# Half rows of a projection weight on 128 partitions, one output DMA, three idle products

## The chip, the cores and the metric

The kernel runs on one core of one Trainium2 chip. Its five engines are TensorE (PE), VectorE (DVE), ScalarE (ACT), GpSimd (POOL) and SyncE (SP); 16 DMA engines move data between HBM and the on-chip memory SBUF. The metric is the device time of one execution in microseconds (us), as the median of several runs.

## The reference

Two independent problems, A and B, are computed, and their outputs are laid side by side. Each is one decode step of attention over the last 4,096 positions of a cache, with a projection before and one behind it. All inputs are bf16.

```python
B, Sq, D = 2, 1, 576
Hq, Hkv, Sk, Dh = 32, 16, 16384, 128
W = 4096
q = (x @ wq).reshape(B, Sq, Hq, Dh).transpose(0, 2, 1, 3)      # wq: 576 x 4096
k = repeat(k_cache[:, :, Sk - W:, :], 2, axis=1)               # 16 heads, each used by two of q
v = repeat(v_cache[:, :, Sk - W:, :], 2, axis=1)
p = softmax(einsum("bhqd,bhkd->bhqk", q, k) * Dh ** -0.5)
o = einsum("bhqk,bhkd->bhqd", p, v)
out = o.transpose(0, 2, 1, 3).reshape(B, Sq, Hq * Dh) @ wo     # wo: 4096 x 576
return concatenate([out_A, out_B], axis=-1)
```

For one query position a head, nearly all bytes are those of K and V: 16 slabs of K and 16 of V, 4 MB each. With wq and wo of both problems the kernel reads 153 MB.

## The kernel before, in words

**Slabs and the ring.** `stream` is the order in which big loads are issued: wq of A and of B, then K and V slabs by turns. A slab is 128 partitions of 32 KB, and `ring` has 4 slots. `issue_slab` puts one slab on SyncE's DMA queue; from the fifth on, SyncE first waits until the last reader of the slot is done (`reader`). The loads of wo (`issue_wo`) go between them on the same queue; the last V slab is cut in two (`PIECES`), and the last rows of wo go out in three DMAs (`issue_last`, semaphores `wl_sem`) behind it. The outputs follow last.

**The order of work.** The Python code adds operations to one list for each engine (`S.add(engine, function, dependencies, tag)`). Each engine runs its list in order. Dependencies become semaphore waits in front of an operation, and those that an earlier wait already covers are dropped. Nothing is reordered, so the order of the calls in the code is the order on the engine.

**The q phase.** wq has 576 rows. Of these, 512 are loaded as a slab in which partition p holds rows 4p to 4p+3 (four chunks), and the last 64 (`DREM`) go into `wqr`. Before the change, row r of problem P lies in partition 2r+P, 8 KB each (L248), so that both problems together fill 128 partitions; `x_dup` holds each of x's last 64 values twice, with zeros (by `maskP`) where the partition belongs to the other problem (L361). `f_xT` (L355) transposes x, chunk by chunk, on PE into a bank of PSUM, and `f_xev` (L369) spreads it into `xT` on ACT. `do_qpair` (L421, with repeated weights L170) then runs the products of q for two groups of heads at a time: 5 chunks by 4 banks, four times. `do_qrow` evicts them on ACT (L435, L440), DVE and ACT rearrange them, and GpSimd builds `zq`, the weights of the score products.

**Steady state.** For each K slab DVE transposes it in four parts (L485), PE makes scores (L510), maxima and exponentials follow on DVE, PE and ACT, and PE multiplies the V slab of an earlier step (L601).

**The tail.** The last V slab comes in two pieces. Between and behind its products PE runs idle products into a bank that is no longer read (`idle_out`): two behind `redist` by `do_redist(D_ // 2, 2)`, and two by `keep_on(2)`, the first of them L729, the others L170. Then come the combination of the accumulator (L648), a normalisation on DVE (L683), the last products with wo (L760; `fin_ops` is a DVE copy, L783, that they wait for), and two copies to `out_sb` (`do_E`: ACT L792 for the lower half of the columns, DVE L793 for the upper). `do_out` (L801) issues the output: A's rows from SyncE long before, B's lower half from ACT and its upper half from SyncE. SyncE then waits until all outputs have landed (L955).

Of the kernel before, what the change touches and what calls it, by code (L numbers as in the profile page):

```python
# [6 lines left out]
BF16 = mybir.dt.bfloat16  # L7
ACTF = mybir.ActivationFunctionType
ALU = mybir.AluOpType
AX = mybir.AxisListType  # L10
# [49 lines left out]
def build_kernel(nc, probs, out, cfg=None):  # L60
    cfg = dict(cfg or {})
    NR = cfg.get("NR", 4)
# [26 lines left out]
    HH = HD // 2  # L89
    NXC = NFC + 1  # L90
    NOUT = wo0.shape[1]
# [15 lines left out]
    with es:  # L107
        sb = lambda name, shape, dt: es.enter_context(nc.sbuf_tensor(name, shape, dt))
        ring = sb("ring", [128, NR, SLABW], BF16)
        xt = sb("xt", [128, NKT, 2048], FP32)  # L110
        wqr = sb("wqr", [128, HD], BF16)
        wob = sb("wob", [128, 2, 8, NOUT], BF16)
        xT = sb("xT", [128, NXC, NPROB, 128], BF16)
        x_dup = sb("x_dup", [NPROB * Bb, DREM, NPROB], BF16)
        maskP = sb("maskP", [NPROB * Bb, NPROB], BF16)
        x_sb = sb("x_sb", [NPROB * Bb, D], BF16)
# [45 lines left out]
        wo_sem = [sem("wo%d" % r) for r in range(2)]  # L162
        x_sem = [sem("xload%d" % P) for P in range(NPROB)]
        wl_sem = [sem("wl%d" % n_) for n_ in range(len(HEADS))]
# [19 lines left out]
        def load_x(P, eng):  # L184
            return dma_op(eng, x_sem[P], 1, lambda e: e.dma_start(
                x_sb[P * Bb:(P + 1) * Bb, :], probs[P][0][:, 0, :]).then_inc(x_sem[P], 16), [], "xload%d" % P)
        x_dma = {0: load_x(0, "act")}
# [56 lines left out]
        def issue_wq(n, P):  # L244
            wqP = probs[P][3]
            r = n % NR
            deps = [reader[n - NR]] if n >= NR else []
            wq_dma[P] = dma_op("sp", wq_sem, 1, lambda e: e.dma_start(  # L248
                wqr[P::NPROB, :], wqP[NFC * 128:D, :]).then_inc(wq_sem, 16), [], "wqr%d" % P)
            slab_dma[n] = dma_op("sp", ring_sem[r], 1, lambda e: e.dma_start(  # L250
                ring[:, r, :], wqP[0:NFC * 128, :].rearrange("(p s) n -> p (s n)", s=NFC)).then_inc(ring_sem[r], 16), deps, "wq%d" % P)

            if P == 0:
                for P_ in range(1, NPROB):
                    x_dma[P_] = load_x(P_, "sp")
# [90 lines left out]
        def f_xT(e, bank):  # L346
            last = None
            bb = bank[:].bitcast(BF16)
            NB = NPROB * Bb
            for ch in range(NXC):  # L350
                if ch < NFC:
                    src = x_sb[0:NB, 0:NFC * 128].rearrange("b (p s) -> b s p", s=NFC)[:, ch, :]
                else:
                    src = x_dup[0:NB, :, :].rearrange("b r t -> b (r t)")
                last = e.transpose(bb[:, ch * NB:(ch + 1) * NB], src, ident_b[0:NB, 0:NB])  # L355
            return last
        issue_until(0)
        init_small()
        init["maskP"] = S.add("dve", lambda e: e.tensor_reduce(
            maskP[:], ident_b[0:NPROB * Bb, 0:NPROB * Bb].rearrange("d (p b) -> d p b", b=Bb), AX.X, ALU.max), [p_ident_b], "maskP")  # L360
        x_cd = S.add("dve", lambda e: e.tensor_tensor(  # L361
            x_dup[:], x_sb[:, NFC * 128:D].unsqueeze(2).broadcast_to([NPROB * Bb, DREM, NPROB]),
            maskP[:].unsqueeze(1).broadcast_to([NPROB * Bb, DREM, NPROB]), ALU.mult), [init["maskP"]] + list(x_dma.values()), "xdup")

        n_x, bank_x, op_xT = tb_job(f_xT, "xT", list(x_dma.values()) + [x_cd, p_ident_b])

        def f_xev(e):
            NB = NPROB * NXC
            return e.activation(  # L369
                xT[:].rearrange("c h p (a w) -> c (h p) a w", a=4)[:, :, :, 0:Bb],  # L370
                bank_x[:].bitcast(BF16)[:, 0:NB * Bb].rearrange("c (p b) -> c p b", b=Bb).unsqueeze(2).broadcast_to([128, NB, 4, Bb]),
                ACTF.Copy)
        op_xev = S.add("act", f_xev, [op_xT, p_zxT], "xev")
        tb_consumer[n_x] = op_xev

# [20 lines left out]
        def do_qpair(i):  # L396
# [4 lines left out]
            banks = q_banks(i)  # L401
            order = [NFC] + list(range(NFC))
            if Gs[0] % GPP:
                order = order[::-1]
            todo_ = [(ch, b) for ch in order for b in range(4)]
            seen = {b: 0 for b in range(4)}
# [3 lines left out]
            for g in range(2):  # L410
                def fn(e, part=todo_[(0, ends[0])[g]:ends[g]]):
                    last = None
                    for ch, b in part:
                        c0 = (b % 2) * HH + 512 * (Gs[b // 2] % GPP)
                        w_ = ring[:, nq % NR, ch * HD + c0:ch * HD + c0 + 512] if ch < NFC else wqr[:, c0:c0 + 512]
                        start, stop = seen[b] == 0, seen[b] == NFC
                        seen[b] += 1
                        if q_first[0] == (P, ch):
                            last = matmul_again(e, q_first[1], banks[b], w_, start, stop, False)
                        else:  # L420
                            last = q_first[1] = e.matmul(banks[b], xT[:, ch, P, :], w_, start=start, stop=stop)  # L421
                            q_first[0] = (P, ch)
                    return last
                op = S.add("pe", fn, [slab_dma[nq], op_xev] + list(wq_dma.values()) + prev, "q%d" % Gs[g])
                reader[nq] = op
                q_done[Gs[g]] = op
# [268 lines left out]
        def do_redist(G, idle=0):  # L695
# [14 lines left out]
            if idle:  # L710
                def f_idle(e):
                    r = None
                    for _ in range(idle):
                        r = matmul_again(e, last[0], idle_out, maskB[:, :], True, True)
                    return r
                S.add("pe", f_idle, [chain[(ND - 1, "exp")], init["maskB"]], "idle%d" % G)
            redist[G] = op
# [7 lines left out]
        fin_ops = []  # L725

        def keep_on(n):
            def f(e):
                first = last = e.matmul(idle_out, ident_b[:, :], maskB[:, :], start=True, stop=True)  # L729
                for _ in range(n - 1):  # L730
                    last = matmul_again(e, first, idle_out, maskB[:, :], True, True)
                return last
            S.add("pe", f, [chain[(ND - 1, "exp")], init["maskB"]], "keep%d" % n)

# [146 lines left out]
        do_PV(D_, range(PIECES[0][0] // JR, PIECES[0][1] // JR), pieces[0])  # L881
        do_redist(D_ // 2, 2)
        do_PV(D_, range(PIECES[1][0] // JR, PIECES[1][1] // JR), pieces[1])
        keep_on(2)
        do_comb(D_)
# [3 lines left out]
        do_E(NPROB - 1)  # L889
        for P in range(NPROB - 1):  # L890
            do_out(P, 0, NOUT, "sp", [e_ops[(P, 0)], e_ops[(P, 1)]])
        do_out(NPROB - 1, 0, NH, "act", [e_ops[(NPROB - 1, 0)]])
        do_out(NPROB - 1, NH, NOUT, "sp", [e_ops[(NPROB - 1, 1)]])

# [99 lines left out]
```

## Time and profile before

| what | value |
|---|---|
| time, median of 3 runs (lowest to highest) | 363.33 us (363.29 to 363.35) |
| the profiled execution's own time | 363.62 us |
| its span, from the first instruction to the last | 362.3 us |
| read from HBM | 153.10 MB, 423 GB/s over the span |
| busy: PE, DVE, ACT, POOL | 224.9, 201.5, 68.7, 35.3 us |
| mean granted clock of TensorE | 0.863 |
| issue to landing: wqr of A, wq of A, wqr of B | 3.7, 12.8, 13.2 us |
| issue to landing: K slabs of A, V slabs of A (median) | 30.8, 32.1 us |

The profile is of one execution. A row of a timeline gives the start and the duration in us, the engine, the line, what is written and read, and in brackets how long the engine was idle before it and what ended that. "SPq" and "ACTq" are DMA issues; "PEld" is the load of a weight into PE. The granted clock is the share of full speed at which TensorE is let run. A row of the windows view gives a stretch, its length, then the busy time of PE, PE's weight loads, DVE, ACT and POOL (each with a count), the granted clock, the share of the DMA engines' time and GB/s. The trace also keeps one record for each DMA packet: its start, its duration and its bytes.

### The profile page before, as it was taken

What the parts mean: (1) busy time and instruction counts of PE and PEld (TensorE: products, weight loads), DVE (VectorE), ACT (ScalarE), POOL (GpSimd) and SP (SyncE); (2) the same over time, 40 slices, a digit from 0 to 9 for tenths busy, and PEclk for the clock granted to TensorE, in tenths of its full rate; (3) what the DMA queues carried; (4) which work ended last, traced back from release to release, by engine and by line L of the source; (5) the groups of instructions that cost most, each with busy time, mean ns of one, the idle gap of its engine ahead of it and who ended that gap; (6) DMA issues with size and microseconds to landing.
All of it is one profiled execution on the core that took longest, in us unless ns stands there. A gap on an engine that the chain in (4) does not pass through costs nothing.

```text
span 362.3 us, 2755 instructions
## 1 busy us (share of the span) xinstructions
PE 224.9 (62%) x1325; PEld 57.4 (16%) x950; DVE 201.5 (56%) x175; ACT 68.7 (19%) x153; POOL 35.3 (10%) x55
## 2 busy tenths in 40 slices
PE   0399195474865647584774747575673738656775
PEld 0000021111221201111121112111121112211121
DVE  3013598483917467291936648092854839179831
ACT  1036402020300303020210203112020203002131
POOL 1000000004000040004000040001200040110020
PEclk9999589788796968889787889969697887969999
DMA  8999999999999999999999999999999999999996
GB/s 348 405 445 423 445 408 433 456 412 442 420 426 434 434 409 447 430 438 430 402 454 430 434 434 418 434 434 430 421 434 430 438 425 430 430 434 434 425 419 242
DMA packets 6943, 153.27 MB, mean 423 GB/s; under 512 B 778, under 2 KB 1300, under 8 KB 1428
## 3 DMA queue, kind: packets, MB, share of 16 engines
q1 hardware_dynamic: 6924, 153.10, 98.7%
q8 instruction: 9, 0.15, 0.2%
q14 instruction: 2, 0.02, 0.0%
q10 hardware_dynamic: 8, 0.00, 0.0%
HBM read 153.10 MB, written 0.00 MB: 423 GB/s over the span
## 4 chain that ended last, share of the span: by engine, by line
DMA 71%; DVE 14%; PE 13%; SPq 1%; issue 0%
DMA ring<-in_B_k_cache_dram 34%; DMA ring<-in_A_k_cache_dram 26%; DVE xt L485 13%; DMA wob<-in_B_wo_dram 8%; PE st L170 6%; DMA wqr<-in_B_wq_dram 4%; PE st L510 4%; PE st L421 1%; PE tb L170 1%; PE acc L170 1%; PE ot L170 1%; DVE nM L533 1%; PE tb L421 0%; PE tb L523 0%; SPq L237 0%
## 5 line engine op out<-in xcount | busy, mean ns | idle before, releaser
L485 DVE STREAM_TRANSPOSE xt<-ring 128x2048 f32<-128x2048 f32 x64 | 145.3, 2285 | 77.3 <-DMA ring<-in_B_k_cache_dram 40.1
L510 PE MATMUL st<-xt,zq 128*128 128x512 bf16 x256 | 115.8, 452 | 114.5 <-DVE xt L485 88.8
L170 PE MATMUL st<-xt,zq 128*128 128x512 bf16 x256 | 114.4, 447 | 0.0
L510 PEld LDWEIGHTS st<-xt,zq 128*128 128x128 bf16 x256 | 27.9, 109 | 210.0 <-DVE xt L485 104.1
L601 PE MATMUL acc<-ring,pC 128*32 128x512 bf16 x512 | 33.9, 381 | 2.6 <-DMA ring<-in_B_v_cache_dram 2.6
L538 ACT ACTIVATE nMrep<-nM 1x128 f32<-1x128 f32 x16 | 4.9, 308 | 142.9 <-DVE nM L533 142.9
L613 ACT ACTIVATE acc_sb<-acc 128x512 bf16<-128x512 f32 x16 | 9.5, 597 | 81.3 <-PE acc L601 81.3
L563 DVE STREAM_TRANSPOSE pC<-pR 128x1024 bf16<-128x1024 bf16 x16 | 19.5, 1216 | 3.6 <-ACT pR L555 2.1
L520 DVE TENSOR_REDUCE m<-st 128x1 f32<-128x1024 f32 x16 | 19.0, 1190 | 1.2 <-PE st L170 1.2
L620 POOL TENSOR_TENSOR acc_sb<-acc_sb,maskJ 128x1024 bf16<-128x1024 bf16 (+1 forms) x8 | 13.4, 1679 | 59.0 <-ACT acc_sb L613 59.0
L472 POOL TENSOR_TENSOR zq<-qk,maskA 128x128 bf16<-128x128 bf16 x16 | 6.3, 399 | 127.9 <-PE st L170 106.1
L555 ACT ACTIVATE pR<-st,bias_sb 128x1024 bf16<-128x1024 f32 x16 | 17.8, 1114 | 0.5
L445 DVE STREAM_TRANSPOSE qtr<-qrow 128x512 f32<-128x512 f32 x8 | 5.7, 712 | 20.8 <-ACT qrow L435 13.5
L387 ACT ACTIVATE st<-maskB 128x1024 f32<-128x1024 bf16 x16 | 16.5, 1032 | 1.6 <-POOL rsel L570 0.4
L756 PE MATMUL ot<-wob,Rsb 128*2 128x512 bf16 x56 | 15.7, 399 | 0.2 <-ACT Rsb L721 0.2
L601 PEld LDWEIGHTS acc<-ring,pC 128*32 128x32 bf16 x512 | 12.9, 95 | 16.1 <-DMA ring<-in_B_v_cache_dram 3.6
L570 POOL TENSOR_TENSOR rsel<-maskS,rsum 128x16 f32<-128x16 bf16 x8 | 1.7, 216 | 124.1 <-ACT pR L555 124.1
L170 PE MATMUL tb<-wob,Rsb 128*2 128x64 bf16 x56 | 11.1, 197 | 0.0
L355 PE MATMUL tb<-ident_b,x_sb 4*128 4x4 bf16 x4 | 0.3, 173 | 14.6 <-DVE x_dup L361 14.6
L775 DVE TENSOR_TENSOR o_rest<-o_rest,tb 2x64 f32<-2x64 f32 x3 | 0.6, 209 | 15.4 <-PE tb L170 15.4
L623 POOL TENSOR_TENSOR acc_sb<-acc_sb 128x512 bf16<-128x512 bf16 (+1 forms) x8 | 8.2, 1030 | 0.6
L533 DVE TENSOR_REDUCE nM<-tb 1x8 f32<-1x128 f32 x16 | 4.4, 272 | 6.2 <-PE tb L523 6.1
(88 smaller groups left out, 107.0 us busy)
## 6 DMA issues: line engine op xcount, KB each, us to landing
ring<-in_A_k_cache_dram SPq DMA_DIRECT2D x8, 4096.0 KB, 30.8
ring<-in_A_v_cache_dram SPq DMA_DIRECT2D x8, 4096.0 KB, 32.1
ring<-in_B_k_cache_dram SPq DMA_DIRECT2D x8, 4096.0 KB, 30.7
ring<-in_B_v_cache_dram SPq DMA_DIRECT2D x7, 4096.0 KB, 32.8
wob<-in_A_wo_dram SPq DMA_DIRECT2D x4, 1152.0 KB, 33.5
ring<-in_A_wq_dram SPq DMA_DIRECT2D x1, 4096.0 KB, 12.8
ring<-in_B_wq_dram SPq DMA_DIRECT2D x1, 4096.0 KB, 22.4
wob<-in_B_wo_dram SPq DMA_DIRECT2D x3, 1152.0 KB, 34.6
```

The costliest lines, as they stand in the source:

```text
L170: return e.add_instruction(mybir.InstMatmult(name=nc.get_next_instruction_name(), engine=i.engine, ins=[e.lower_ap(rhs), i.ins[1]], outs=[ ...
L387: chain[(s, "fill")] = S.add("act", lambda e: e.activation(ST[s % 2][:, :].rearrange("k (h j) -> k h j", h=2), maskB[:].unsqueeze(1).broad ...
L485: Xop[(s, u)] = S.add("dve", lambda e: e.transpose(xt[:, i % NKT, :].rearrange("k (j w) -> k j w", w=64), ring[:, n % NR, :].bitcast(FP32) ...
L510: first = last = e.matmul(bank, zq[:, p4, s % NZQ, w0:w0 + 128], mv, start=False, stop=stop, skip_group_check=True)
L520: chain[(s, "max")] = S.add("dve", lambda e: e.tensor_reduce(m1[:, 0:1], ST[s % 2][:, :], AX.X, ALU.max), d, "max%d" % s)
L555: chain[(s, "exp")] = S.add("act", lambda e: e.activation(pR[:, :], ST[s % 2][:, :], ACTF.Exp, bias=bias_sb[:, 0:1], scale=SCALE, accum_ou ...
L563: chain[(s, "pC")] = S.add("dve", lambda e: e.transpose(pC[:, s % NPT, :, :].rearrange("k j c -> k (j c)"), pR[:, :]), d, "pC%d" % s)
L601: last = e.matmul(ACC[32 * cb:32 * cb + 32, 0:512], pC[:, D_ % NPT, j0_:j0_ + 4, :].rearrange("k j c -> k (j c)"), ring[:, n % NR, j0_ * 1 ...
L613: acc_ev[D_] = S.add("act", lambda e: e.activation(acc_sb[:, D_ % 2, :], ACC[:, :], ACTF.Copy), d, "accev%d" % D_)
L620: t = S.add("pool", lambda e: e.tensor_tensor(v, v, maskJ[:].unsqueeze(1).unsqueeze(3).broadcast_to([128, l1 - l0, 4, 128]), ALU.mult), [a ...
L623: t = S.add("pool", lambda e: e.tensor_tensor(a_[:, :, 0:256], a_[:, :, 0:256], a_[:, :, 256:512], ALU.add), [t], "acca%d" % D_)
L756: first = e.matmul(OT[0:Bb, 0:NB0], l_, wob[:, pc, s_, 0:NB0], start=start and begin, stop=end, skip_group_check=True)
```

## The change

- `wqr` gets a place of its own for each problem. A row of wq's last 64 is split into two halves of 4 KB, which lie in partitions 2r and 2r+1; a DMA fills 128 partitions with 4 KB each instead of 64 with 8 KB.
- x gets a sixth chunk instead of a mask between the problems: chunk 4 is zero in the odd partitions and chunk 5 in the even ones, so that chunk 4 makes the lower half of q's columns and chunk 5 the upper half. `x_dup` becomes a plain doubling copy, `f_xT` writes products with a repeated identity (16 columns each), ACT evicts four chunks, and a new DVE product with `maskP` writes the other two (`f_xev2`). One semaphore counts both loads of x.
- In `do_qpair` the second product group of a pair also waits until all banks of the pair before are evicted (`before`).
- `keep_on` is gone; the idle products behind the last `redist` are three and wait for `fin_ops`.
- B's output leaves by one DMA from SyncE, which waits for both copies.

```diff
@@ -87,7 +87,7 @@
     DREM = D - 128 * NFC
     assert DREM * 2 == 128 and NFC * HD == SLABW
     HH = HD // 2
-    NXC = NFC + 1
+    NXC = NFC + 2
     NOUT = wo0.shape[1]
     NH = NOUT // 2
     NB0 = 512
@@ -108,11 +108,11 @@
         sb = lambda name, shape, dt: es.enter_context(nc.sbuf_tensor(name, shape, dt))
         ring = sb("ring", [128, NR, SLABW], BF16)
         xt = sb("xt", [128, NKT, 2048], FP32)
-        wqr = sb("wqr", [128, HD], BF16)
+        wqr = sb("wqr", [128, NPROB, HH], BF16)
         wob = sb("wob", [128, 2, 8, NOUT], BF16)
         xT = sb("xT", [128, NXC, NPROB, 128], BF16)
-        x_dup = sb("x_dup", [NPROB * Bb, DREM, NPROB], BF16)
-        maskP = sb("maskP", [NPROB * Bb, NPROB], BF16)
+        maskP = sb("maskP", [128, 2], BF16)
+        x_dup = sb("x_dup", [NPROB * Bb, DREM, 2], BF16)
         x_sb = sb("x_sb", [NPROB * Bb, D], BF16)
         ident_b = sb("ident_b", [128, 128], BF16)
         zq = sb("zq", [128, 4, NZQ, ZW], BF16)
@@ -160,7 +160,7 @@
         ring_sem = [sem("ring%d" % r) for r in range(NR)]
         wq_sem = sem("wq")
         wo_sem = [sem("wo%d" % r) for r in range(2)]
-        x_sem = [sem("xload%d" % P) for P in range(NPROB)]
+        x_sem = sem("xload")
         wl_sem = [sem("wl%d" % n_) for n_ in range(len(HEADS))]
         out_sem = sem("outdone")
         piece_sem = [sem("piece%d" % n_) for n_ in range(NPC)]
@@ -182,8 +182,8 @@
             return op
 
         def load_x(P, eng):
-            return dma_op(eng, x_sem[P], 1, lambda e: e.dma_start(
-                x_sb[P * Bb:(P + 1) * Bb, :], probs[P][0][:, 0, :]).then_inc(x_sem[P], 16), [], "xload%d" % P)
+            return dma_op(eng, x_sem, 1, lambda e: e.dma_start(
+                x_sb[P * Bb:(P + 1) * Bb, :], probs[P][0][:, 0, :]).then_inc(x_sem, 16), [], "xload%d" % P)
         x_dma = {0: load_x(0, "act")}
 
         p_ones_b = S.add("pool", lambda e: e.memset(ones_b[:], 1.0), [], "ones_b")
@@ -246,7 +246,7 @@
             r = n % NR
             deps = [reader[n - NR]] if n >= NR else []
             wq_dma[P] = dma_op("sp", wq_sem, 1, lambda e: e.dma_start(
-                wqr[P::NPROB, :], wqP[NFC * 128:D, :]).then_inc(wq_sem, 16), [], "wqr%d" % P)
+                wqr[:, P, :], wqP[NFC * 128:D, :].rearrange("r (h n) -> r h n", h=2)).then_inc(wq_sem, 16), [], "wqr%d" % P)
             slab_dma[n] = dma_op("sp", ring_sem[r], 1, lambda e: e.dma_start(
                 ring[:, r, :], wqP[0:NFC * 128, :].rearrange("(p s) n -> p (s n)", s=NFC)).then_inc(ring_sem[r], 16), deps, "wq%d" % P)
 
@@ -345,32 +345,39 @@
 
         def f_xT(e, bank):
             last = None
-            bb = bank[:].bitcast(BF16)
             NB = NPROB * Bb
-            for ch in range(NXC):
+            for ch in range(NFC + 1):
                 if ch < NFC:
                     src = x_sb[0:NB, 0:NFC * 128].rearrange("b (p s) -> b s p", s=NFC)[:, ch, :]
                 else:
                     src = x_dup[0:NB, :, :].rearrange("b r t -> b (r t)")
-                last = e.transpose(bb[:, ch * NB:(ch + 1) * NB], src, ident_b[0:NB, 0:NB])
+                last = e.matmul(bank[:, ch * 4 * NB:(ch + 1) * 4 * NB], src, ident_b[0:NB, 0:NB].rearrange(
+                    "k (p b) -> k p b", b=Bb).unsqueeze(2).broadcast_to([NB, NPROB, 4, Bb]), start=True, stop=True)
             return last
         issue_until(0)
         init_small()
+        x_cd = S.add("dve", lambda e: e.tensor_copy(
+            x_dup[:], x_sb[:, NFC * 128:D].unsqueeze(2).broadcast_to([NPROB * Bb, DREM, 2])), list(x_dma.values()), "xdup")
         init["maskP"] = S.add("dve", lambda e: e.tensor_reduce(
-            maskP[:], ident_b[0:NPROB * Bb, 0:NPROB * Bb].rearrange("d (p b) -> d p b", b=Bb), AX.X, ALU.max), [p_ident_b], "maskP")
-        x_cd = S.add("dve", lambda e: e.tensor_tensor(
-            x_dup[:], x_sb[:, NFC * 128:D].unsqueeze(2).broadcast_to([NPROB * Bb, DREM, NPROB]),
-            maskP[:].unsqueeze(1).broadcast_to([NPROB * Bb, DREM, NPROB]), ALU.mult), [init["maskP"]] + list(x_dma.values()), "xdup")
+            maskP[:], ident_b[:].rearrange("d (r t) -> d t r", t=2), AX.X, ALU.max), [p_ident_b], "maskP")
 
         n_x, bank_x, op_xT = tb_job(f_xT, "xT", list(x_dma.values()) + [x_cd, p_ident_b])
 
         def f_xev(e):
-            NB = NPROB * NXC
+            NB = NPROB * NFC * 4
             return e.activation(
-                xT[:].rearrange("c h p (a w) -> c (h p) a w", a=4)[:, :, :, 0:Bb],
-                bank_x[:].bitcast(BF16)[:, 0:NB * Bb].rearrange("c (p b) -> c p b", b=Bb).unsqueeze(2).broadcast_to([128, NB, 4, Bb]),
+                xT[:, 0:NFC].rearrange("c h p (a w) -> c (h p a) w", a=4)[:, :, 0:Bb],
+                bank_x[:, 0:NB * Bb].rearrange("c (q b) -> c q b", b=Bb),
                 ACTF.Copy)
         op_xev = S.add("act", f_xev, [op_xT, p_zxT], "xev")
+        NB_ = NPROB * 4 * Bb
+
+        def f_xev2(e):
+            return e.tensor_tensor(
+                xT[:, NFC:NXC].rearrange("c h p (a w) -> c h (p a) w", a=4)[:, :, :, 0:Bb],
+                bank_x[:, NFC * NB_:(NFC + 1) * NB_].rearrange("c (q b) -> c q b", b=Bb).unsqueeze(1).broadcast_to([128, 2, NPROB * 4, Bb]),
+                maskP[:].unsqueeze(2).unsqueeze(3).broadcast_to([128, 2, NPROB * 4, Bb]), ALU.mult)
+        op_xev = S.add("dve", f_xev2, [op_xev, op_xT, init["maskP"]], "xev2")
         tb_consumer[n_x] = op_xev
 
         def init_mask():
@@ -399,10 +406,11 @@
             nq = pos[("Q", P)]
             issue_until(pos[("Q", NPROB - 1)])
             banks = q_banks(i)
-            order = [NFC] + list(range(NFC))
+            mine = lambda ch: [b for b in range(4) if ch < NFC or b % 2 == ch - NFC]
+            order = [NFC, NFC + 1] + list(range(NFC))
             if Gs[0] % GPP:
                 order = order[::-1]
-            todo_ = [(ch, b) for ch in order for b in range(4)]
+            todo_ = [(ch, b) for ch in order for b in mine(ch)]
             seen = {b: 0 for b in range(4)}
             prev = [q_free.get((i - 2, b)) for b in range(4)]
             ends = [max(n for n, (ch, b) in enumerate(todo_) if b // 2 == g) + 1 for g in range(2)]
@@ -412,7 +420,7 @@
                     last = None
                     for ch, b in part:
                         c0 = (b % 2) * HH + 512 * (Gs[b // 2] % GPP)
-                        w_ = ring[:, nq % NR, ch * HD + c0:ch * HD + c0 + 512] if ch < NFC else wqr[:, c0:c0 + 512]
+                        w_ = ring[:, nq % NR, ch * HD + c0:ch * HD + c0 + 512] if ch < NFC else wqr[:, P, c0 - (b % 2) * HH:c0 - (b % 2) * HH + 512]
                         start, stop = seen[b] == 0, seen[b] == NFC
                         seen[b] += 1
                         if q_first[0] == (P, ch):
@@ -421,7 +429,8 @@
                             last = q_first[1] = e.matmul(banks[b], xT[:, ch, P, :], w_, start=start, stop=stop)
                             q_first[0] = (P, ch)
                     return last
-                op = S.add("pe", fn, [slab_dma[nq], op_xev] + list(wq_dma.values()) + prev, "q%d" % Gs[g])
+                before = [q_free.get((i - 1, b)) for b in range(4)] if g else []
+                op = S.add("pe", fn, [slab_dma[nq], op_xev] + list(wq_dma.values()) + prev + before, "q%d" % Gs[g])
                 reader[nq] = op
                 q_done[Gs[g]] = op
 
@@ -713,7 +722,7 @@
                     for _ in range(idle):
                         r = matmul_again(e, last[0], idle_out, maskB[:, :], True, True)
                     return r
-                S.add("pe", f_idle, [chain[(ND - 1, "exp")], init["maskB"]], "idle%d" % G)
+                S.add("pe", f_idle, [chain[(ND - 1, "exp")], init["maskB"]] + fin_ops, "idle%d" % G)
             redist[G] = op
             deps = [op, wo_dma[G]] if by_group(G) else [op]
             if G >= 2:
@@ -723,14 +732,6 @@
             tb_consumer[n] = r_ev[G]
 
         fin_ops = []
-
-        def keep_on(n):
-            def f(e):
-                first = last = e.matmul(idle_out, ident_b[:, :], maskB[:, :], start=True, stop=True)
-                for _ in range(n - 1):
-                    last = matmul_again(e, first, idle_out, maskB[:, :], True, True)
-                return last
-            S.add("pe", f, [chain[(ND - 1, "exp")], init["maskB"]], "keep%d" % n)
 
         def fin(half):
             return ST[(ND - 2) % 2][32 * half:32 * half + Bb, 512 * half:512 * half + NH]
@@ -879,18 +880,15 @@
         D_ = ND - 1
         issue_until(len(stream) - 1)
         do_PV(D_, range(PIECES[0][0] // JR, PIECES[0][1] // JR), pieces[0])
-        do_redist(D_ // 2, 2)
+        do_redist(D_ // 2, 3)
         do_PV(D_, range(PIECES[1][0] // JR, PIECES[1][1] // JR), pieces[1])
-        keep_on(2)
         do_comb(D_)
         do_norm(D_)
         do_proj(ND - 2)
         do_proj(D_)
         do_E(NPROB - 1)
-        for P in range(NPROB - 1):
+        for P in range(NPROB):
             do_out(P, 0, NOUT, "sp", [e_ops[(P, 0)], e_ops[(P, 1)]])
-        do_out(NPROB - 1, 0, NH, "act", [e_ops[(NPROB - 1, 0)]])
-        do_out(NPROB - 1, NH, NOUT, "sp", [e_ops[(NPROB - 1, 1)]])
 
         S.check()
 
```

## The prediction

> **What bounds the kernel now.** I read the page first: the span, the row of DMA shares in 40 slices, and the queues.
>
> ```profile
> span 362.3 us, 2755 instructions
> ...
> DMA  8999999999999999999999999999999999999996
> ...
> q1 hardware_dynamic: 6924, 153.10, 98.7%
> ```
>
> The 16 DMA engines are busy in every slice between the first and the last. SyncE's queue alone fills 98.7% of 362.3 us, that is 357.6 us. In the trace's packet records its first packet starts at 2.28 us and its last weight packet ends at 359.96, a stretch of 357.7 us: the engines never pause. So three things make the time: when the first packet starts, how long all the packets take, and what follows the last one. Next, what SyncE's queue waits for:
>
> ```profile
> SPq L241 <- DVE xt L485: 185.5, 14, 14.8
> SPq L241 <- PE acc L170: 29.5, 2, 22.0
> SPq L955 <- DMA out_dram<-out_sb: 1.0, 1, 1.0
> ```
>
> Those waits are for a free ring slot, and they are no loss. A 4 MB slab lands about 31 us after its issue but takes about 9.7 us to move (8 packets on each engine of 1,213 ns), so some 20 us of earlier transfers lie queued ahead of each new one. Then the start, by the timeline:
>
> ```profile
> 0.80 0.56 SPq L248 DMA_DIRECT2D wqr<-in_A_wq_dram  x1
> 2.41 0.48 SPq L248 DMA_DIRECT2D wqr<-in_B_wq_dram  x1
> ...
> 14.91 0.24 ACT L369 ACTIVATE xT<-tb 128x80 bf16<-128x80 bf16 x1 [12.24 <-PE tb L355]
> 15.70 0.58 PE L421 MATMUL st<-wqr,xT 128*128 128x512 bf16 x1 [0.82 <-DMA wqr<-in_B_wq_dram]
> ```
>
> The q products wait for B's half of wqr, not for x: xT is written by 15.15. And the end:
>
> ```profile
> 356.57 0.38 PE L170 MATMUL st<-maskB,om 128*128 128x512 bf16 x1
> 357.37 0.61 PE L601 MATMUL acc<-ring,pC 128*32 128x512 bf16 x8 [0.42 <-DMA ring<-in_B_v_cache_dram]
> 357.92 0.39 PE L729 MATMUL st<-maskB,ident_b 128*128 128x512 bf16 x1
> ...
> 358.69 0.26 PE L648 MATMUL tb<-ident_r,acc_sb 128*128 128x8 bf16 x4 [0.17 <-ACT acc_sb L613]
> ...
> 360.25 0.08 PEld L760 LDWEIGHTS st<-wob,oTn 128*2 128x2 bf16 x2 [0.28 <-DMA wob<-in_B_wo_dram]
> ...
> 361.01 0.26 ACTq L801 DMA_DIRECT2D out_dram<-out_sb  x1
> 361.06 0.27 SPq L801 DMA_DIRECT2D out_dram<-out_sb  x1
> ```
>
> The last two products wait 0.28 us for the last rows of wo, and the two before them 0.20 us. The end hangs on the last weight transfer, then 0.3 us of products, 0.45 of copies and an output transfer of about 1 us.
>
> **The change, part by part.** The profiled execution took 363.62 us (its span is 362.3); the median of the runs is 363.33, 0.29 less. I carry every difference from the one to the other unchanged.
>
> *Packets of wqr.* Two transfers of 64 packets of 8,192 bytes become two of 128 packets of 4,096. In the packet records a packet of 8,192 bytes takes 309 ns undisturbed and one of 32,768 takes 1,213: 0.0368 ns a byte plus 7.7 ns a packet (the same line gives 50.1 for 1,152 bytes, which took 51). Each engine gets 4 more packets in each of two transfers: 8 x 7.7 = +0.06 us, on the path, since the engines never pause. [...]
>
> *Start of the first transfer.* It now issues 128 rows where it had 64. Nothing in the trace shows a 128-row transfer into empty queues. Two rows bound it. SyncE's issue doesn't grow with rows: 0.56 us for these 64, 0.57 for the 128 of wq behind it, so nothing. But the 16 engines start their first packets at 2.28 to 2.63, 0.35 us from first to last, or 5.5 ns a row if they are fed row by row; twice the rows would make the last engine 0.35 later. Below zero: the 64 first-transfer packets average 396 ns against 309, 0.35 us an engine, and a start in smaller pieces might lose less. So -0.35 to +0.35, with more under the rivals. I take +0.17, midway between the two rows, as neither is nearer. B's wqr transfer is queued behind 11 us of others, so its feeding is hidden.
>
> *The x chain.* The copy to x_dup loses its mask operand (before: 0.28 us); the five PE instructions stay five, 16 columns wide instead of 4 (160 to 173 ns at 4); the ACT eviction handles 64 elements instead of 80 (0.24). New behind it is a DVE product of 128x32 elements: between 0.17 us (the 128x8 product, L683) and 0.43 (the 128x256 one, L674), plus a hop of 0.05. xT would be ready at 15.35 to 15.65, while B's wqr lets PE start at 15.70, later still with the two terms above. Uncovered, at most 0.1. maskP moves behind the copy and is not waited for before that product; maskC and maskB move some 0.5 us later and are first read at 33.35. The larger clear of xT (+0.1) has until 14.9.
>
> *Q products.* Still 80, with 4 more weight loads of 0.1 us, which run beside the products as the others do. The second product group of each pair now also waits for the evictions of the pair before. For pairs 1 and 2 these end 1 us and 0.6 us earlier than the products that wait. For the last pair, the eviction L435 runs from 34.35 to 35.35, and the last product stood at 35.08: +0.3. Queued behind it on PE are the score products, which start at 43.90 for X's sake; waiting for it is SyncE with K2's issue at 35.49. The first four slabs and both wqr are 17.8 MB, 41 us of transfers, and V0 and wo, issued at 27, add 12 more: the engines have work until about 55. Even 15 us later would cost nothing.
>
> *The tail on PE.* Of the four idle products two went behind the last V piece (357.92 to 358.5), where PE waits for ACT's eviction until 358.64: taking them away gains nothing. The third one put ahead of that piece ends at about 356.57 + 3 x 0.215 = 357.2, and the piece lands for 357.37. Uncovered, 0.2, which the 0.20 and 0.28 us of waiting for wo swallow. The new wait there is for a DVE copy that ended at 353.84; behind it on PE stands the last V piece, which waits longer for its data.
>
> *Output.* One issue instead of two. ACT's copy ends at 360.98 and DVE's at 361.03, so SyncE issues at 361.06 as now, with rows of 1,152 bytes (51 ns) instead of 576 (30): +0.02. Bounds: -0.05 (SyncE's issue took 0.92 us to its first packet beside ACT's 0.87) and +0.05 for the second wait.
>
> The sum: 0.06 + 0.17 + 0.02 = +0.25 us. That makes the profiled execution 363.87 and the median **363.6**.
>
> **The rivals.**
>
> *The feeding decides (slower).* Transfers of 2 rows took 0.51 (x) and 0.61 and 0.64 us (out) from the end of their issue to the first packet, that of 64 rows 0.92. On that line 64 more rows hold back the first packet by 0.28 to 0.42, and the last engine by the 0.35 on top: up to +0.77, with 0.08 for the rest 364.2 (+0.23%). It decides if the first wqr packet starts after 2.6. Against it: x's transfer was issued at the same moment, which alone could explain a late 0.92.
>
> *The clock falls in the tail (slower, smaller).* The windows view, cut at the edges where the granted clock changes, has
>
> ```profile
> 140.05:143.46 3.41, 1.43 (x9) 0.39 (x4) 2.23 (x2) 0.75 (x2) 0.00 (x0) 0.98 0.96 410
> 351.67:355.08 3.41, 1.55 (x16) 0.48 (x13) 0.61 (x2) 0.36 (x1) 0.00 (x0) 1.00 0.86 364
> 358.50:361.91 3.41, 1.73 (x21) 0.72 (x20) 0.62 (x2) 0.54 (x2) 0.00 (x0) 0.98 0.20 69
> ```
>
> After the first and the third the clock was halved, after the second not. So 1.4 to 1.7 us of busy PE in 3.41 is near the limit, and the change takes a net 0.21 us of products out of the tail. At half clock the last 16 products, 288 columns in pairs, would cost 8 x 0.12 = 0.96 more, less the 0.48 of waits: +0.5, and 364.1. Against it: in this phase the window 355.08 to 358.50 keeps about 2.6 us. [...]
>
> *128 partitions pay (faster).* If the 0.35 us of the first transfer goes, the sum is -0.35 + 0.06 + 0.02 = -0.27: 363.1. For it, only those long first packets. Against a larger gain: B's wqr on 64 partitions averages 320 ns a packet, and the last V piece on 128 partitions takes 313, so the half-filled layout already moves at nearly full rate. [...]
>
> *Something the trace does not show* (another packet rate, another order of landings): half a per cent either way.
>
> **How the numbers follow.** A measurement of this kernel can tell about 0.2%, or 0.73 us, from no change: faster means below 362.60, slower above 364.06. Chances: the sum 0.60 (363.3 to 363.9, within 0.2%); feeding 0.13, of which 0.09 ends above the line; clock 0.06, half of it above; 128 partitions 0.12, all within; unseen 0.09, 0.06 of it faster and 0.03 slower. That makes 0.06 faster, 0.79 same and 0.15 slower. The range 363.0 to 364.2 takes in the first four but for the ends of feeding and clock.
>
> **What would show it.** In the changed profile: wqr packets of about 158 ns; the first at 2.3 with the engines' starts spread over up to 0.7 us; q products at 15.7 to 16.0, behind DMA and not DVE; the last wo rows releasing PE at about 360.4 to 360.5 instead of 360.25; full clock until then; one output issue right behind the copies. I am wrong if the DMA share falls anywhere between the ends, if PE in the tail waits for anything but transfers, or if wqr's packets differ from 158 ns by more than a fifth.

## The result, and the profile after

| | before | after |
|---|---|---|
| median (runs) | 363.65 us (22) | 364.56 us (22) |
| ratio, 95% interval | | 1.0022 [1.0016, 1.0029] |
| profiled execution, its span | 363.62, 362.3 us | 364.58, 363.2 us |
| granted clock, mean | 0.863 | 0.861 |

The change costs 0.9 us: slower, where I had forecast 363.6, too small a difference to tell from none. (A ratio is worked out from undisturbed runs alone, so it is not exactly the quotient of the two medians.) The spans show it more sharply: 363.0 to 363.5 us in all runs of after, 361.9 to 362.7 in the 73 runs of before beside the experiments. The page of after:

```profile
span 363.2 us, 2756 instructions
...
DMA  8999999999999999999999999999999999999994
...
q1 hardware_dynamic: 7052, 153.10, 98.4%
q8 instruction: 9, 0.15, 0.2%
```

SyncE's queue fills 98.4% of 363.2, 357.4 us, as much as before (357.6). The transfers are no longer; but the last slice is 4 where it was 6, so something comes later behind them. The start, from the timeline:

```profile
0.80 0.40 SPq L248 DMA_DIRECT2D wqr<-in_A_wq_dram  x1
...
15.01 0.19 DVE L376 TENSOR_TENSOR xT<-tb,maskP 128x32 bf16<-128x32 f32 x1 [0.48 <-ACT xT L368]
...
15.32 0.59 PE L429 MATMUL st<-wqr,xT 128*128 128x512 bf16 x1 [0.61 <-DVE xT L376]
```

The issue of A's wqr takes 0.40 us instead of 0.56, and in the packet records its first packet starts at 1.83 instead of 2.15 and the last engine has finished it at 3.83 instead of 4.14. The q products start 0.38 us earlier. So the head gained 0.3 us. (The packet times in the prediction, 2.28 to 2.63 and 359.96, are 0.13 us too late against the timeline; before's stretch is 2.15 to 359.83. The delays from an issue to its first packet, 0.51 to 0.92, are 0.13 too long for the same reason. Differences between packet times, and between those delays, stand. All packet times here have the timeline's zero.) The tail, from the timeline:

```profile
355.81 0.81 PE L170 MATMUL st<-maskB,om 128*128 128x512 bf16 x2
...
356.82 0.61 PE L610 MATMUL acc<-ring,pC 128*32 128x512 bf16 x8 [0.21 <-DMA ring<-in_B_v_cache_dram]
...
358.32 0.66 PE L761 MATMUL st<-wob,Rsb 128*2 128x288 bf16 x8
...
360.49 0.98 PE L761 MATMUL st<-wob,oTn 128*2 128x288 bf16 x8 [1.51 <-DMA wob<-in_B_wo_dram]
...
361.07 0.08 PEld L761 LDWEIGHTS st<-wob,oTn 128*2 128x2 bf16 x2 [0.23 <-DMA wob<-in_B_wo_dram]
361.51 0.40 ACT L793 ACTIVATE out_sb<-st 2x288 bf16<-2x288 f32 x1 [3.43 <-PE st L761]
361.51 0.45 DVE L794 CAST out_sb<-st 2x288 bf16<-2x288 f32 x1 [2.92 <-PE st L761]
362.06 0.26 SPq L802 DMA_DIRECT2D out_dram<-out_sb  x1
```

(Of the three idle products, the first row, two left a record.) The last V piece comes 0.55 us earlier than before (356.82 against 357.37). But then PE waits 1.51 us for wo's last rows, and its last weight load is released at 361.07 instead of 360.25. The output's issue is 1.00 us later: 0.82 from wo, 0.11 because the last products take 0.44 us to the copies instead of 0.33, and 0.07 because SyncE starts 0.10 us after both copies where it had started 0.03 after its own. The 0.11 is the clock, which was at 1.00 in before from 360.00 to the copies. In after, by the windows view cut around the end:

```profile
360.00:361.00 1.00, 0.51 (x6) 0.20 (x6) 0.00 (x0) 0.00 (x0) 0.00 (x0) 0.99 0.04 14
361.00:361.50 0.50, 0.45 (x4) 0.08 (x2) 0.00 (x0) 0.00 (x0) 0.00 (x0) 0.50 0.00 0
```

**Which transfer is late.** The packet records give each DMA engine's end of a transfer as a record of 4 bytes, 16 for each large transfer. In after, wo's last rows have landed on all but one engine by 359.25; three such records follow at 359.55, 360.22 and 360.60, the ends of three transfers. In before the last come at 359.73 and 359.83. So one engine is 1.35 us behind the others. What does it do? The row q8 of the page is the answer: nine packets of 16 KB on a queue called "instruction". They are PE's, as e1 shows (with 56 PE instructions fewer there are eight), and the same 16 engines carry them, as the landings below show. The first eight come 34 to 48 us apart, the ninth 17 us behind the eighth in before and 18 in after, and each takes 0.96 to 1.26 us. Between one and the next PE starts 246 to 272 products and weight loads, on average 259 in before's records and 256 in after's. In after the ninth lasts from 358.23 to 359.31, and from 359.30 on the records have one packet of wo at a time, those of a single engine. The landings of single slabs in before, in us behind the first of 16 engines, around the first such fetch (60.27) and behind the eighth (342.81):

```
landed by  54.0:  0 to 0.5, all 16
landed by  67.9:  0 to 0.5, 15 engines;  1.9, one engine
landed by 347.1:  0 to 0.8, 8 engines;   1.6 to 2.0, 8 engines
```

Every fetch puts one engine about 1.4 us behind, until eight are late. (The records name no engine. But in before the slabs that land behind the first, second and further fetches have exactly 1, 2, 3 and so on to 8 landings that are 1.6 us or more behind the first one, so it is another engine each time.) The ninth fetch starts at 359.73 in before, when wo's rows are nearly all in, and at 358.23 in after, ahead of them.

**The theory (fetch).** The next 16 KB are asked for a little after PE passes a fixed place of its program. (Places are counted in the kernel's list of PE instructions; a product that loads its weight is two.) The ninth place lies at about 2211, and the first product of the last V piece, which has to wait for its data, stands at 2209 in before and at 2213 in after (ahead of it, four weight loads in the q phase and one idle product more, and one instruction less that only waits). In before the fetch is asked for behind that wait; in after ahead of it, 1.5 us earlier, and an engine that is late already is held up once more while it still has wo's rows to bring. No row shows PE waiting for instructions; what waits is the data behind the fetch on its engine (PE 1.51 us for wo's last rows in after).

Rivals: the clock falls in the tail and makes it longer; the half rows cost time at the start; the output's single issue or the separate wait costs it.

### The profile page after: what moved, and what is told of

The parts are those of the page before. It is cut to its first block, busy times and chain, and to the rows that moved or that the text cites. A ratio compares the mean times of both kernels' runs of the same rounds, so it can differ in the third digit from the quotient of the medians.

```text
span 363.2 us, 2756 instructions
## 1 busy us (share of the span) xinstructions
PE 227.4 (63%) x1324; PEld 58.4 (16%) x953; DVE 201.8 (56%) x176; ACT 68.7 (19%) x153; POOL 35.3 (10%) x55
## 3 DMA queue, kind: packets, MB, share of 16 engines
q1 hardware_dynamic: 7052, 153.10, 98.4%
## 4 chain that ended last, share of the span: by engine, by line
DMA 72%; DVE 16%; PE 8%; ACT 3%; SPq 1%; issue 0%
DMA ring<-in_B_k_cache_dram 34%; DMA ring<-in_A_k_cache_dram 26%; DVE xt L494 14%; DMA wob<-in_B_wo_dram 8%; PE st L170 4%; DMA x_sb<-in_B_x_dram 3%; PE st L519 3%; ACT qrow L444 1%; DVE qtr L454 1%; ACT qk L462 1%; PE st L429 1%; DVE nM L542 1%; ACT qrow L449 1%; PE tb L532 0%; SPq L237 0%
## 5 line engine op out<-in xcount | busy, mean ns | idle before, releaser
L610 PE MATMUL acc<-ring,pC 128*32 128x512 bf16 x512 | 36.0, 401 | 1.1 <-DMA ring<-in_B_v_cache_dram 1.1
L558 ACT ACTIVATE bias_sb<-tb 128x1 f32<-128x1 f32 x16 | 2.7, 171 | 26.0 <-PE tb L552 26.0
```

The source lines that it names most:

```text
L610: last = e.matmul(ACC[32 * cb:32 * cb + 32, 0:512], pC[:, D_ % NPT, j0_:j0_ + 4, :].rearrange("k j c -> k (j c)"), ring[:, n % NR, j0_ * 1 ...
```

## The experiments

Before was measured again beside the experiments, three times, at medians of 363.52, 363.45 and 363.53 us. "Place" is that of the last V piece's first product; the records of the ninth fetch and of wo's last landing, and PE's last release, are from each profile.

| kernel | place | 9th fetch | wo landed | PE released | median | ratio [95%] |
|---|---|---|---|---|---|---|
| e1_after_cut56 | 2157 | none | 359.79 | 360.22 | 363.16 | 0.9989 [0.9980, 0.9999] |
| before | 2209 | 359.73 | 359.83 | 360.25 | 363.5 | 1 |
| e8_before_late8 | 2209 | 360.44 | 359.73 | 360.17 | 363.60 | 1.0001 [0.9991, 1.0011] |
| e4_tail_out_only | 2210 | 359.34 | 359.66 | 360.11 | 363.55 | 0.9997 [0.9988, 1.0007] |
| e5_after_idle0 | 2210 | 359.17 | 359.45 | 359.89 | 363.44 | 0.9999 [0.9989, 1.0010] |
| e10_wqr_idle0 | 2210 | 359.22 | 359.34 | 359.77 | 363.29 | 0.9991 [0.9978, 1.0004] |
| e7_before_pad2 | 2211 | 359.48 | 359.48 | 360.01 | 363.47 | 0.9996 [0.9986, 1.0005] |
| e6_before_pad3 | 2212 | 358.22 | 360.94 | 361.40 | 364.74 | 1.0030 [1.0019, 1.0041] |
| e3_wqr_only | 2212 | 358.21 | 360.82 | 361.31 | 364.60 | 1.0026 [1.0016, 1.0037] |
| after | 2213 | 358.23 | 360.60 | 361.07 | 364.56 | 1.0022 [1.0016, 1.0029] |
| e2_before_pad8 | 2217 | 358.39 | 361.11 | 361.56 | 364.84 | 1.0029 [1.0013, 1.0045] |
| e9_before_pad130 | 2339 | 352.38 | 361.17 | not by wo | 365.85 | 1.0056 [1.0036, 1.0077] |

**e1: after, 56 PE instructions fewer.** Seven of eight rounds of the first V slab of A are left out, so the output is incomplete.

```diff
...
-                    do_PV(c, range(NRD), None)
+                    do_PV(c, range(7 if c == 0 else 0, NRD), None)
```

> The changed kernel with 56 PE instructions fewer: seven of the eight rounds of the first V slab of problem A are left out (28 products and their 28 weight loads), 290 us before the end. Theory 'fetch': in the changed kernel the ninth fetch of 16 KB of PE's instructions (one every 256 instructions) reaches its DMA engine at 358.2 us, ahead of 1.3 us of wo's last rows, where before it came at 359.7, behind them. 56 instructions fewer put it off beyond the last products: the last rows of wo release PE at about 359.5 instead of 361.07, and the time is about 363.0, that is 1.5 below the changed kernel and 0.5 below the kernel before, because the first transfer starts earlier. Theory 'feed' (128 rows cost time at the start): no change, 364.5. Theory 'clock' (PE runs at half speed in the tail because idle products are gone): no change, 364.5.

363.16. The page and the timeline:

```profile
q8 instruction: 8, 0.13, 0.1%
```

```profile
360.22 0.08 PEld L761 LDWEIGHTS st<-wob,oTn 128*2 128x2 bf16 x2 [0.27 <-DMA wob<-in_B_wo_dram]
```

With eight fetches wo's last rows release PE at 360.22 again, with half rows, tail and output as in after. I had expected 359.5 and 363.0; the profiled execution, 363.56, was the longest of the ten, so its rows say little about that difference. By itself this leaves open whether the fetch or the work left out matters; the next one reverses it.

**e2: before, 8 PE instructions more at its start**, a weight load and seven small products that run at 1.42 to 1.76 us, when PE has nothing else.

```diff
+        def f_pad(e):
+            first = last = e.matmul(TB[1][:, 0:4], ident_b[:, :], ident_b[:, 0:4], start=True, stop=True)
+            for _ in range(6):
+                last = matmul_again(e, first, TB[1][:, 0:4], ident_b[:, 0:4], True, True)
+            return last
+        S.add("pe", f_pad, [p_ident_b], "pad")
```

> The kernel before with 8 more PE instructions (one weight load and seven products of 4 columns into a free bank) at about 2 us, where PE is idle. Theory 'fetch': the ninth fetch moves 8 instructions earlier in the program, from behind the wait for the last V piece to ahead of it, so it starts near 358.5 instead of 359.7 and holds back one engine's rows of wo by some 1.3 us: about 364.8, with the last rows releasing PE at 361.4 instead of 360.25. Theories 'feed' and 'clock': nothing that matters has changed, 363.4 to 363.7.

364.84: 1.3 us for eight instructions that nobody waits for, some 355 us before the place where they cost. The timeline has after's tail in a kernel that has nothing of the change:

```profile
360.92 0.93 PE L767 MATMUL st<-wob,oTn 128*2 128x288 bf16 x8 [1.59 <-DMA wob<-in_B_wo_dram]
...
361.56 0.08 PEld L767 LDWEIGHTS st<-wob,oTn 128*2 128x2 bf16 x2 [0.28 <-DMA wob<-in_B_wo_dram]
```

**e3 and e4: the change in two.** e3 has the half rows, the sixth chunk and `before` in `do_qpair`, with the tail and the outputs of before; e4 has the tail and the single output alone.

```diff
 e3, against after
-                S.add("pe", f_idle, [chain[(ND - 1, "exp")], init["maskB"]] + fin_ops, "idle%d" % G)
+                S.add("pe", f_idle, [chain[(ND - 1, "exp")], init["maskB"]], "idle%d" % G)
...
-        do_redist(D_ // 2, 3)
+        do_redist(D_ // 2, 2)
...
+        keep_on(2)
...
-        for P in range(NPROB):
+        for P in range(NPROB - 1):
             do_out(P, 0, NOUT, "sp", [e_ops[(P, 0)], e_ops[(P, 1)]])
+        do_out(NPROB - 1, 0, NH, "act", [e_ops[(NPROB - 1, 0)]])
+        do_out(NPROB - 1, NH, NOUT, "sp", [e_ops[(NPROB - 1, 1)]])
```

> The kernel before with the half rows, the doubled chunk and the new wait in the q products, but the old tail (two idle products and two behind the last V piece) and the old two output DMAs. The four new weight loads move the last V piece from place 2209 to 2212 of PE's program. Theory 'fetch': the fetch is ahead of the piece as in the changed kernel, 364.4; its start gains 0.3 to 0.5 us as there. Theory 'feed': it holds all the loss, 364.5, with a start no earlier than before. Theory 'clock': 363.5, as the idle products are back.

> The kernel before with only the new tail (three idle products, none behind the last V piece) and the single output DMA. The last V piece stands at place 2210 of PE's program, one later than before. Theory 'fetch': if one place is not enough to bring the fetch ahead of the wait for the piece, 363.5 with 0.1 for the output; if it is, 364.8. Theory 'feed': 363.5. Theory 'clock': most of the loss, 364.3, with the granted clock halved before the last products.

364.60 and 363.55: the whole loss is in e3, whose part beside PE's count is a gain at the head. Its three PE instructions more (four weight loads, one wait less) are enough. The timelines, e3 first:

```profile
360.66 0.94 PE L769 MATMUL st<-wob,oTn 128*2 128x288 bf16 x8 [1.37 <-DMA wob<-in_B_wo_dram]
```

```profile
360.11 0.08 PEld L752 LDWEIGHTS st<-wob,oTn 128*2 128x2 bf16 x2 [0.29 <-DMA wob<-in_B_wo_dram]
```

So the tail with three idle products, the separate wait and the single output cost nothing that shows, as predicted. Nor is the clock the cause: e2, e3 and e6 wait 1.59, 1.37 and 1.44 us for wo, like after, and from PE's last release to the copies their last products take 0.33 us, as in before, and not 0.44 as in after.

**e5: after without the three idle products** (place 2210).

```diff
-        do_redist(D_ // 2, 3)
+        do_redist(D_ // 2, 0)
```

> The changed kernel without its three idle products behind the last redistribution: the last V piece's first product moves from place 2213 of PE's program to 2210. Theory 'fetch': as 2210 stayed fast with the new tail alone and 2212 was slow with the half rows alone, the ninth fetch is asked for only once the piece has landed; it starts some 2.1 us later, at about 359.3, behind nearly all rows of wo: 363.2, below the kernel before by 0.3 (the first transfer starts 0.3 us earlier). Theory 'clock': without any idle product PE falls to half speed before the last products, 364.5 to 365. Theory 'feed': 364.5 as before.

363.44. The timeline:

```profile
359.24 0.93 PE L761 MATMUL st<-wob,oTn 128*2 128x288 bf16 x8
...
359.89 0.08 PEld L761 LDWEIGHTS st<-wob,oTn 128*2 128x2 bf16 x2 [0.27 <-DMA wob<-in_B_wo_dram]
```

Taking work out of the tail, which by the clock theory makes it worse, takes 1.18 us off PE's last release. The products run at full clock (1.00 granted from 355 us on; 0.93 us for the eight, 0.94 in before). I had expected 363.2, 0.3 below before, for the earlier head; that gain does not show here, 363.44 against before's 363.45.

**e6 and e7: the edge.** e2's pad with one product behind the first (three instructions) and with none (two).

> The kernel before with three more PE instructions at about 2 us (one weight load, two products of 4 columns): the last V piece at place 2212. Theory 'fetch': 2212 lies beyond the point, so the whole loss comes back, 364.8, though 3 instructions of under 0.1 us each were added to an idle engine. Any other theory: 363.5.

> The kernel before with two more PE instructions at about 2 us (one weight load, one product): the last V piece at place 2211, between the fast 2210 and the slow 2212. Theory 'fetch': either 363.5 or 364.8 and nothing between, which finds the point exactly. Any other theory: 363.5.

364.74 and 363.47: one product on an idle engine, at 1.5 us, is worth 1.27 us at the end. The timelines, e6 first:

```profile
360.76 0.93 PE L767 MATMUL st<-wob,oTn 128*2 128x288 bf16 x8 [1.44 <-DMA wob<-in_B_wo_dram]
```

```profile
360.01 0.29 PE L767 MATMUL st<-wob,oTn 128*2 128x288 bf16 x2 [0.17 <-DMA wob<-in_B_wo_dram]
```

**e8: e2's eight instructions behind the last V piece** instead of at the start.

```diff
         do_PV(D_, range(PIECES[1][0] // JR, PIECES[1][1] // JR), pieces[1])
+        def f_late(e):
+            first = last = e.matmul(idle_out[:, 0:4], ident_b[:, :], ident_b[:, 0:4], start=True, stop=True)
+            for _ in range(6):
+                last = matmul_again(e, first, idle_out[:, 0:4], ident_b[:, 0:4], True, True)
+            return last
+        S.add("pe", f_late, [chain[(ND - 1, "exp")]], "late")
         keep_on(2)
```

> The kernel before with the same 8 more PE instructions as in the padded kernel (one weight load and seven products of 4 columns), but behind the last V piece instead of at the start; the piece stays at place 2209. Theory 'fetch': the fetch is still asked for behind the piece's wait, 363.5; the extra products lie beside ACT's eviction. If it were the number of instructions in all that counts, or the work of the added products: 364.8 as with the padding at the start.

363.60. The same instructions, as many, and no loss: what counts is how many stand ahead of the wait.

```profile
360.17 0.08 PEld L760 LDWEIGHTS st<-wob,oTn 128*2 128x2 bf16 x2 [0.28 <-DMA wob<-in_B_wo_dram]
```

**e9: e2's pad with 128 products behind the first**, so that the ninth fetch leaves wo's rows alone.

> The kernel before with 130 small products more in front of the transposes of x (into a bank that nothing reads yet), so that the last fetch of PE's instructions falls some 130 places earlier in its program, near 346 us, in the middle of the last slabs, and no fetch falls among wo's last rows. If the fetch costs because it stands directly ahead of wo's last rows on an engine that is already late, the time is that of before, 363.3 to 363.6, with PE released for the last products at 360.0 to 360.3. If it is enough that one engine has two fetches behind each other anywhere, the delay of 1.3 us stays with that engine to the end and the time is 364.6 to 364.9. If more instructions as such are slow, it is slower than all kernels so far: above 364.9.

365.85, slower than all: none of the three was right as written. The fetch came at 352.38 and not at 346: its place lies among the products of the V slab before the last, which PE starts only at 348.08. Of the 16 engines, 15 had landed V's first piece by 354.85 and one at 355.75 (in before all by 354.40), and one engine, by this the same, still brought wo's last rows at 361.17, where before's came at 359.83. So a second fetch on a late engine stays with it to the end, as the second branch had it. That the time is above that branch's, and in the third's, the timeline and the windows of e9 show:

```profile
356.25 2.40 PE L608 MATMUL acc<-ring,pC 128*32 128x512 bf16 x24 [2.33 <-DMA ring<-in_B_v_cache_dram]
...
359.60 0.83 PE L608 MATMUL acc<-ring,pC 128*32 128x512 bf16 x8
```

```profile
356.50:358.50 2.00, 2.00 (x24) 0.60 (x16) 0.00 (x0) 0.00 (x0) 0.00 (x0) 0.54 0.98 379
358.50:360.00 1.50, 1.50 (x12) 0.27 (x10) 0.00 (x0) 0.18 (x1) 0.00 (x0) 0.50 0.58 208
```

V's first piece starts at 356.25 instead of 354.88, and after the wait of 2.33 us the clock is halved: its 24 products take 2.33 us to the next one instead of 1.41. PE, not wo, then bounds the tail, with the last V piece at 359.60 instead of 357.37. Here the clock rival is real, as a second cost of a late transfer. 1.37 us of lateness and 0.92 of clock make 2.3; some of it comes back, as the last products no longer wait for wo, and the outputs issue 1.92 us later than before's (profiled executions: 365.52 against 363.62; the median of four runs is 2.3 above before's). That 130 instructions cost nothing in another way was not tested apart.

**e10: half rows, with before's outputs and two idle products behind the last piece, none ahead of it** (place 2210).

```diff
 against before, beside the half rows
-        do_redist(D_ // 2, 2)
+        do_redist(D_ // 2, 0)
```

> The half rows of the change with the outputs and the separate wait of before, and no idle products behind the first piece: the last piece's first product stands at place 2210, so the fetch comes behind the wait for it. By the fetch theory it has the earlier start of the half rows without the late fetch: 363.1 to 363.4, 0 to 0.4 us below before. If the half rows themselves cost time (0.06 us of packets, a slower start), 363.5 to 363.8. If the idle products are needed to keep the clock up, 364.0 or more.

363.29. The timeline at the start and at the end:

```profile
15.38 0.59 PE L429 MATMUL st<-wqr,xT 128*128 128x512 bf16 x1 [1.01 <-DMA wqr<-in_B_wq_dram]
...
359.77 0.08 PEld L769 LDWEIGHTS st<-wob,oTn 128*2 128x2 bf16 x2 [0.27 <-DMA wob<-in_B_wo_dram]
```

In this profile wo's last rows release PE 0.48 us earlier than in before's, and the median is 0.24 us lower. (e3 is as much below e2, 364.60 against 364.84; both have the late fetch and were measured together.) The interval, 0.9978 to 1.0004, does not exclude no change, and e5 showed none. e10's is the lowest median of the kernels that do the whole work, and 1.3 us below after.

## Why the prediction was wrong, step by step

**What bounds it: right, and incomplete.** The end does hang on the last weight transfer, and in every kernel here but e9 PE's last release follows wo's last landing by 0.42 to 0.53 us. But "how long all the packets take" is not the same for the 16 engines. The row that says so was on the page of before, one line below the one that I quoted:

```profile
q8 instruction: 9, 0.15, 0.2%
```

0.2% of 16 engines' span reads as nothing. It is 0.2% of the sum, but each packet falls on one engine: nine times about 1.1 us of packet, and the last engine sets the time.

**The step that failed: the PE instructions costed at nothing.** "4 more weight loads of 0.1 us, which run beside the products" and "the third one put ahead of that piece" were weighed as PE's time only, and as that they are free: the piece's first product still waited for DMA (0.21 us), and the third idle product ended at 356.62, ahead of it. As places in PE's program they move the ninth fetch by 1.5 us and cost 1.2 (after's release at 361.07 against 359.89 in e5). The prediction had no term for this, and the chance of 0.03 for a slower result that the trace does not show was the only part that held it; the trace did show it.

**The start of the first transfer: wrong sign.** I took +0.17, midway between 0 and +0.35. Measured: -0.32 at the first packet, which starts at 2.14 to 2.16 in the seven profiles with 64 rows and at 1.83 to 1.84 in all five with 128. The lower bound, -0.35, was near, though not for its reason: the first transfer's packets still average 179 to 203 ns against 159 for B's, but they started earlier, with a shorter issue (0.40 against 0.56 us). The bound "SyncE's issue doesn't grow with rows" was thus on the wrong side too: this one shrank.

**Packets of wqr: right.** A packet of 4,096 bytes takes 159 ns, 158 predicted, so 7.7 ns a packet holds. The term of 0.06 us is too small to show in the whole: wo's last rows land 357.50, 357.62 and 357.97 us after the first packet in e10, e5 and e1, and 357.68 in before.

**The x chain: right in size.** The new DVE product takes 0.19 us (0.17 to 0.43 predicted). In after PE waited for it and not for wqr, as B's half came earlier; in e3, e5 and e10 it waited for wqr at 15.38 to 15.42.

**Q products: the wait right.** The last product stood 0.25 us for the eviction (0.3 predicted), and SyncE's queue waits for slots as before:

```profile
SPq L241 <- DVE xt L494: 182.5, 14, 14.6
SPq L241 <- PE acc L610: 77.5, 13, 8.0
SPq L241 <- PE ot L170: 29.1, 2, 21.3
```

**Tail on PE, output:** the idle products and the wait for `fin_ops` cost nothing, as e4 and e5 show. The output took 0.07 us more at its issue against 0.02 predicted, a little above the upper bound of 0.05.

**The rivals.** Feeding came within 0.4 us of the measured time, by the wrong mechanism: its own sign, a first packet after 2.6, did not come. The clock was worth 0.11 us in after and nothing in e2, e3 and e6 with waits as long. "128 partitions pay", at -0.27, is near the 0.24 of e10 in size, if that is real, but it came by an earlier start and not by shorter first packets. Of the signs under "What would show it", three failed: the first packet at 1.83 instead of 2.3, the q products at 15.32 behind DVE instead of 15.7 to 16.0 behind DMA, and wo's rows releasing PE at 361.07 instead of 360.4 to 360.5. Of the signs of being wrong one was there, for another reason: in after's tail PE waits 0.71 us for ACT where two idle products had stood, and that costs nothing, as wo's rows come later. The DMA share does not fall between the ends, and wqr's packets are within 1 ns of 158.

## What to carry to other kernels

Where DMA engines are busy to the end, look at the page's instruction queue and find when its packets start against the last transfers: one instruction more ahead of a late wait can put a fetch of 16 KB ahead of the rows that the end hangs on (here place 2212 instead of 2211 cost 1.27 us). A share of the sum over 16 engines says nothing of the slowest engine (here the row said 0.2%, and one engine was 1.35 us behind); look at the spread of the 16 landings of one transfer. An edit that seems to cost or to gain a microsecond should be tried once more with a few idle instructions put in or taken out, before its own mechanism is believed or dismissed.

## What the runs showed of the hardware that was not expected

- A fetch of PE's instructions (16 KB, 0.96 to 1.26 us a packet in before and after) makes one DMA engine about 1.4 us late, and in the landings of before none of these engines caught up by 347.1; eight fetches made eight engines late, and in after the ninth held back one of these again, whose rows of wo landed 1.35 us behind all others.
- The place that asks for it is sharp: 2211 and 2212 differ by 1.27 us in the time.
- A first transfer of 128 rows of 4 KB starts 0.32 us earlier than one of 64 rows of 8 KB on every second partition, and its issue is 0.16 us shorter. Which of the two properties does it was not tried.
